# Tables for engines and urgencies in an attention and mixture-of-experts kernel

## The chip, the cores and the metric

The kernel runs on one core of one Trainium2 chip. The time is device microseconds of one execution of the whole program, median of several runs; smaller is better. The core has five engines with a queue each, worked off in order: TensorE (PE, matmul; its weight loads are shown as PEld), VectorE (DVE), ScalarE (ACT), GpSimd (POOL) and SyncE (SP, which here only issues DMAs). POOL issues DMAs too, here those that add into their destination. The profile is taken by the hardware profiler in one execution.

## The reference

Attention with 2 batches, 8 heads, 768 positions and 64 columns per head, local windows plus block summaries, then two mixture-of-experts layers. Cut to what matters:

```python
def _attn_ref(q, k, v):                    # each (2, 8, 768, 64)
    block, window = (32, 16)
    k_sum = k.reshape(B, H, nb, block, D).max(axis=3)
    v_sum = v.reshape(B, H, nb, block, D).mean(axis=3)
    scores_l = scale * np.matmul(q, k.transpose(0, 1, 3, 2))     # kept where |i - j| < window
    scores_s = scale * np.einsum('bhsd,bhnd->bhsn', q, k_sum) + np.log(block)
    a = softmax over [scores_l masked, scores_s]
    return np.matmul(a, np.concatenate([v, v_sum], axis=2))

def _moe_ref(x, domain_probs, w1, w2):     # x (1536, 512), 4 experts, 1024 hidden columns
    p = domain_probs / (domain_probs.sum(-1, keepdims=True) + 1e-09)
    for e in range(E):
        out += p[:, e:e + 1] * (np.maximum(x @ w1[e], 0.0) @ w2[e])

def _moe2_ref(x, w_gate, w1, w2):          # the same with 8 experts
    logits = x @ w_gate
    P = np.exp(logits - logits.max())      # then 8 rounds of row and column normalisation
    ...                                    # out += P[:, e:e + 1] * (relu(x @ w1[e]) @ w2[e])
```

Everything is computed in float32 precision: each operand of a large matmul is split into a high part, rounded for the matmul, and a low part, the difference, and three products are added.

## The kernel before, in words

**Stages.** The attention works on 8 pairs of heads, each in 3 groups of 4 windows. Per pair: load keys, queries, values and value windows (`add_loads`, SP's queue), transpose keys and queries on TensorE, copy the key windows out of PSUM, take the block maxima and spread them beside the windows (line 1139, `add_keys`), scale the queries (line 1166, `add_queries`), add up the values of a block (`add_values`). Per group (`add_group`): scores on TensorE (lines 1228 and 1234), row maxima (line 1250) and sums on DVE, exponentials on ACT (line 1256), the product with the reciprocal of the sums on POOL (line 1271), transposes (1280), a copy (1286), the product with the values (1295), a copy (1306). `add_x` turns the attention's result into seven operand combinations of Strassen's scheme with high and low parts (`hi_op`, line 468, on ACT; `lo_op`, lines 458 and 463, on DVE or POOL).

Then 96 steps follow, one for each of 48 quarters of experts (16 in the first layer, 32 in the second) and each half of the rows. A step has seven products of the first matrix (line 306, six matmuls of 384 columns each) and twice seven of the second (line 629, three matmuls each), 84 matmuls in all. Between them `add_hop` makes seven operands with high and low parts, and ACT and DVE empty the PSUM banks and add into accumulators (line 646 and the helpers in lines 241 to 247, which record the lines of `vsub`, `vadd` and `vmul`). Weights are loaded by SP; their combinations are made by casts on ACT (lines 486 and 499), subtractions on DVE and adding DMAs from POOL's queue (lines 502 and 515). At the border between the layers `add_turn` turns accumulators into the second layer's operands, `add_gate` and `add_sinkhorn` compute the gates and `add_scale` applies them, some steps later. At the end `add_out` combines the accumulators, transposes the result on TensorE (line 947), copies it from PSUM to stage buffers (DVE line 955 for odd tiles, ACT line 959 for even ones) and stores it.

**The order.** No instruction is issued where it is written. Each `op` call records an operation with its engine, a duration name, what it reads and writes, and a due time in steps; its number is its place in that order of calls (0 to 8223). At the end `run_work` plans them all: from the operations whose inputs are there in its plan it always takes the one that can start first, and among those that can start at the same time the one with the smallest due time, and issues it. So the order of every engine's queue is fixed when the program is built. The plan's durations are in the table `SPAN` (how long the engine is taken, and when the result is there), `HOP_WAIT` is added where a result goes to another engine, and operations marked as shared (`w[5]`) wait for each other, whether on DVE or on POOL:

```python
                    t = max(f, at[i], port) if w[5] else max(f, at[i])
                    ...
                    key = (t, w[3], i)        # w[3] is the due time
```

The engine of an operation is written out where it is made (`vop` for DVE, `aop` for ACT), with a few lists that move some to POOL: `XPOOL` for low parts in `add_x`, `VPOOL` and `KSPOOL` for pair 7.

Of the kernel before, what the change touches and what calls it, by code (L numbers as in the profile page):

```python
# [12 lines left out]
ALU = mybir.AluOpType  # L13
# [5 lines left out]
def local_global_attention_moe_moe(  # L19
# [299 lines left out]
    def relu(S, out, src, th, neg=False):  # L319
# [35 lines left out]
    HOP_WAIT = 0.12  # L355
# [26 lines left out]
    def run_work():  # L382
# [7 lines left out]
        free, avail, dma = {}, {}, 0.0  # L390
# [9 lines left out]
        for _ in range(n):  # L400
# [47 lines left out]
    def vop(fn, reads, writes, due, span="v", two=True, use=None):  # L448
        op("DVE", span, reads, writes, due, fn, two, use=use)

    def aop(fn, reads, writes, due, span="a", use=None):
        op("ACT", span, reads, writes, due, fn, use=use)

    def lo_op(eng, to, src, reads, writes, due, neg=False):
        def fn(e=nc.gpsimd if eng == "POOL" else nc.vector):
# [9 lines left out]
        op(eng, "p384" if eng == "POOL" else "v", reads, writes, due, fn, True)  # L465

    def hi_op(to, src, reads, writes, due, neg=False):
        aop(lambda: nc.scalar.mul(to(0), src, -1.0 if neg else 1.0), reads, writes, due, "ah")  # L468
# [58 lines left out]
    def add_first(n):  # L527
# [11 lines left out]
        def fork(out, src, kin, kout, due, by=1.0):  # L539
            aop(lambda: nc.scalar.mul(out, src, by), [kin], [kout], due)  # L540

        def gate(name, src, th, reads, due, two, neg=False):
            if plain(S):
                aop(lambda: relu(S, q[name], src, th, neg), reads, [name], due)
# [36 lines left out]
    def add_hop(n):  # L581
# [12 lines left out]
        def two(f, o, x, y, due):  # L594
            vop(lambda: f(q[o], q[x], q[y]), [x, y], [o], due)
# [24 lines left out]
    def add_second(n):  # L620
# [18 lines left out]
        def copy(out, kout, src, kin, due):  # L639
            aop(lambda: nc.scalar.copy(out=out, in_=src), [kin], [kout], due)  # L640
# [79 lines left out]
    def add_x(b, c, due):  # L720
# [7 lines left out]
        def two(f, out, x, y, reads, writes, d):  # L728
            vop(lambda: f(out, x, y), reads, writes, d)
# [23 lines left out]
    def add_turn(b, due):  # L753
        for c in range(KH):
# [13 lines left out]
            def two(f, out, x, y, kx, ky, ko, d):  # L768
                vop(lambda: f(out, x, y), [kx, ky], [ko], d)
# [18 lines left out]
    def add_scale(b, row, due):  # L788
        p0, p1_ = row[:, 0:HB], row[:, HB:BLK]
        for c in range(KH):  # L790
# [4 lines left out]
            def two(f, out, x, y, reads, ko):  # L795
                vop(lambda: f(out, x, y), reads, [ko], due)
# [756 lines left out]
```

## Time and profile before

| | |
|---|---|
| time, median of 3 runs | 1538.95 us (1538.51 to 1541.38) |
| span of the profiled execution | 1537.7 us, 26631 instructions |
| TensorE busy | 1508.6 us, 98% |
| DVE busy | 1376.9 us, 90% |
| ACT busy | 1131.5 us, 74% |
| POOL busy | 480.8 us, 31% |
| granted TensorE clock, mean | 0.997 |

For the profiled execution the page gives the span, from its first instruction to its last; its time outside of the span is not listed. A window row gives, for one stretch, the busy time of each engine with the number of its instructions, the granted clock of TensorE as a share of full speed, the mean busy share of the 16 DMA engines and their GB/s. Matmuls are pipelined, so that a busy TensorE need not be at its peak. In a timeline row the start is in microseconds from the start of the span; the second number is the duration, and behind it stand engine, line, operation, output and input, with the idle time ahead of it and what ended that in brackets. Successive operations of one engine overlap: the next one starts before the shown end of the one before.

### The profile page before, as it was taken

The numbers are of one execution on the slowest core, as the hardware profiler recorded it, in microseconds if no ns is written. First come the engines' busy times: TensorE is split into PE (matmuls) and PEld (weight loads), VectorE is DVE, ScalarE is ACT, GpSimd is POOL, SyncE is SP. The second block draws the span as 40 slices with busy tenths as digits, with TensorE's granted clock in tenths as the row PEclk, the third lists the DMA queues.
The fourth block names the chain that finished last, engine by engine and source line by source line (L and its number), as shares of the span: only waits on it lengthen the run. The fifth ranks groups of instructions, "written<-read, shape, count | busy, mean of one in ns | idle before, by whom it ended". The sixth has DMA issues, their size and how long they took to land.

```text
span 1537.7 us, 26631 instructions
## 1 busy us (share of the span) xinstructions
PE 1508.6 (98%) x9048; PEld 1483.7 (96%) x9048; DVE 1376.9 (90%) x2846; ACT 1131.5 (74%) x2455; POOL 480.8 (31%) x508
## 2 busy tenths in 40 slices
PE   7989999999999999999999999999999999999997
PEld 6779999999999988999999999999999999999997
DVE  7877989899989998999899899899989989989988
ACT  5888777777777788777677777777777767767765
POOL 3443323323322242343332332323323332332220
PEclk9999999999999999999999999999999999999999
DMA  9967667666666684687666666666666667667642
GB/s 222 218 123 136 120 128 133 125 129 119 125 133 121 123 148 80 113 174 144 119 121 136 121 117 131 127 121 126 129 116 132 126 114 138 122 110 140 122 68 90
DMA packets 199865, 197.56 MB, mean 128 GB/s; under 512 B 46496, under 2 KB 158000, under 8 KB 199728
## 3 DMA queue, kind: packets, MB, share of 16 engines
q0 software_dynamic: 83776, 117.47, 48.3%
q1 hardware_dynamic: 115952, 78.39, 18.0%
q8 instruction: 71, 1.16, 0.3%
q14 instruction: 66, 0.54, 0.1%
HBM read 73.97 MB, written 3.22 MB: 50 GB/s over the span
## 4 chain that ended last, share of the span: by engine, by line
PE 90%; DVE 6%; ACT 2%; issue 1%; DMA 0%; POOL 0%; SPq 0%; DVEq 0%; ACTq 0%
PE bank L306 44%; PE bank L629 43%; PE bank L1234 1%; DVE acc L241 1%; DVE hoph L463 1%; DVE acc L1125 0%; DVE acc L244 0%; PE bank L1295 0%; DVE sm L1262 0%; DVE quads L244 0%; DVE xlo L463 0%; DVE quads L323 0%; ACT s L1256 0%; PE bank L1198 0%; DVE xlo L458 0%
## 5 line engine op out<-in xcount | busy, mean ns | idle before, releaser
L629 PE MATMUL bank<-hoph,w2hi 128*128 128x384 f32 x2688 | 686.7, 336 | 5.0 <-ACT bank L640 2.2
L629 PEld LDWEIGHTS bank<-hoph,w2hi 128*128 128x128 f32 x2688 | 483.5, 188 | 10.9 <-ACT bank L640 5.2
L629 PE MATMUL bank<-hoph,w2lo 128*128 128x384 f32 x1344 | 449.3, 334 | 0.4 <-DVE w2lo L244 0.4
L468 ACT ACTIVATE hoph<-quads 128x384 fp32r<-128x384 f32 x672 | 336.9, 520 | 109.1 <-PE bank L629 65.9
L241 DVE TENSOR_TENSOR acc<-bank,acc 128x384 f32<-128x384 f32 x726 | 378.7, 550 | 29.8 <-PE bank L629 29.1
L306 PE MATMUL bank<-xhi,w1hi 128*128 128x384 f32 x1008 | 339.1, 336 | 2.3 <-ACT w1hi L486 1.8
L306 PE MATMUL bank<-xlo,w1hi 128*128 128x384 f32 x1008 | 338.1, 335 | 0.8 <-DVE xlo L463 0.6
L306 PE MATMUL bank<-xhi,w1lo 128*128 128x384 f32 x1008 | 337.6, 335 | 0.4 <-DVE w1lo L244 0.4
L515 POOL DMA_DIRECT2D raw<-raw x195 | 201.0, 1041 | 405.1 <-DMA raw<-raw 181.2
L463 DVE TENSOR_TENSOR hoph<-quads,hoph 128x384 fp32r<-128x384 f32 x582 | 311.5, 550 | 9.2 <-ACT hoph L468 4.5
L629 PEld LDWEIGHTS bank<-hoph,w2lo 128*128 128x128 f32 x1344 | 252.3, 188 | 0.7 <-DVE w2lo L244 0.7
L640 ACT COPY bank<-bank 128x384 f32<-128x384 f32 x384 | 181.4, 472 | 92.6 <-PE bank L629 88.0
L306 PEld LDWEIGHTS bank<-xhi,w1hi 128*128 128x128 f32 x1008 | 189.5, 188 | 4.9 <-ACT w1hi L486 2.1
L306 PEld LDWEIGHTS bank<-xlo,w1hi 128*128 128x128 f32 x1008 | 189.5, 188 | 1.5 <-DVE xlo L463 1.4
L306 PEld LDWEIGHTS bank<-xhi,w1lo 128*128 128x128 f32 x1008 | 189.6, 188 | 0.8 <-DVE w1lo L244 0.7
L640 ACT COPY acc<-bank 128x384 f32<-128x384 f32 x222 | 104.8, 476 | 106.7 <-PE bank L629 104.9
L515 POOL DMA_DIRECT2D xf<-xf x93 | 97.8, 1052 | 187.3 <-DMA xf<-xf 91.9
L502 POOL DMA_DIRECT2D w2lo<-raw x67 | 71.0, 1059 | 153.2 <-ACT w2lo L499 142.3
L599 DVE SCALAR_TENSOR_TENSOR quads<-quads 128x384 f32<-128x384 f32 x192 | 105.7, 551 | 1.6
L323 DVE SCALAR_TENSOR_TENSOR quads<-bank,pb 128x384 f32<-128x384 f32 x180 | 99.5, 553 | 6.2
L244 DVE TENSOR_TENSOR quads<-quads,bank 128x384 f32<-128x384 f32 x96 | 53.1, 553 | 57.4 <-PE bank L306 57.2
L244 DVE TENSOR_TENSOR quads<-quads 128x384 f32<-128x384 f32 x186 | 102.4, 551 | 1.8
(193 smaller groups left out, 1920.7 us busy)
## 6 DMA issues: line engine op xcount, KB each, us to landing
raw<-raw POOLq DMA_DIRECT2D x130, 256.0 KB, 3.8
raw<-in_moe_w_dram SPq DMA_DIRECT2D x66, 256.0 KB, 2.9
raw<-in_moe_w_dram SPq DMA_DIRECT2D x128, 128.0 KB, 2.9
xf<-xf POOLq DMA_DIRECT2D x62, 256.0 KB, 3.8
w2lo<-raw POOLq DMA_DIRECT2D x33, 384.0 KB, 4.9
w1lo<-raw POOLq DMA_DIRECT2D x32, 384.0 KB, 4.0
pb<-prow SPq DMA_DIRECT2D x24, 384.0 KB, 4.0
w2lo<-raw POOLq DMA_DIRECT2D x34, 256.0 KB, 3.8
```

What stands on the lines that cost most here:

```text
L241: (eng or nc.vector).tensor_tensor(out=out, in0=x, in1=y, op=ALU.add)
L244: (eng or nc.vector).tensor_tensor(out=out, in0=x, in1=y, op=ALU.subtract)
L306: nc.tensor.matmul(pm, l[:, s, cs_], x_of(b, c, r, x), start=first and i == 0, stop=i == n - 1, skip_group_check=True,)
L323: nc.vector.scalar_tensor_tensor(out=out, in0=src, scalar=0.0, in1=PB[S[1]][:, th * HB:(th + 1) * HB], op0=ALU.min if neg else ALU.max, op ...
L463: e.tensor_tensor(out=out, in0=src, in1=hi.bitcast(F32), op=ALU.subtract)
L468: aop(lambda: nc.scalar.mul(to(0), src, -1.0 if neg else 1.0), reads, writes, due, "ah")
L502: lambda: nc.gpsimd.dma_start(out=l, in_=src, accum_op=ALU.add),
L515: lambda o=o, x=x: nc.gpsimd.dma_start(out=o, in_=x, accum_op=ALU.add),
L599: nc.vector.scalar_tensor_tensor(out=q[o], in0=q[x], scalar=-1.0, in1=q[y], op0=ALU.mult, op1=ALU.subtract)
L629: nc.tensor.matmul(cut[bank], l[:, s, cols], hop_of(t, r), start=start and i == 0, stop=i == 2, skip_group_check=True,)
L640: aop(lambda: nc.scalar.copy(out=out, in_=src), [kin], [kout], due)
L1234: nc.tensor.matmul(pw[:, tt * KX:(tt + 1) * KX], bd[p][:, g * GT + tt].rearrange("x j q -> x (j q)"), kw[p][(g * GT + tt) // KT][:, (g * G ...
```

## The change

A table `MOVED` gives operations by number a new engine, and a table `SHIFT` adds to the due time of 286 operations (from -80.5 to +84.1 steps). For this `op` takes a list of alternatives (`others`), each with engine, duration name and function, and the helpers that make operations hand one over: a high part or a copy out of PSUM on DVE instead of ACT, a low part or an addition on POOL instead of DVE or the other way, scaled queries and key copies on ACT instead of DVE or the other way, the share product on DVE. The lists `VPOOL` and `KSPOOL` go, and in `add_out` all stage copies are on ACT unless the table names them. With the entries that name the engine an operation has anyway left out, and 4 stage copies added that change for that reason, 180 operations change their engine:

| numbers | where | ACT to DVE | DVE to POOL | DVE to ACT | POOL to DVE |
|---|---|---|---|---|---|
| 0 to 522 | attention | 24 | 17 | 13 | 11 |
| 523 to 755 | steps 0 to 3 | 15 | 4 | | |
| 2869 to 3169 | steps 30 to 33 | 3 | 8 | | |
| 3170 to 3579 | steps 33 to 37 | 17 | 17 | | |
| 3580 to 3921 | steps 38 to 41 | 13 | 20 | | |
| 8043 to 8216 | last steps and end | 6 | 8 | 4 | |

The 24 of the attention are 9 copies of transposed shares, 9 copies of the attention's result, 3 high parts, 2 key copies and one scaling; the 17 are 14 additions and low parts and 3 spreads; the 13 are 6 scalings, 5 key copies and 2 small copies; the 11 are 8 share products and 3 low parts. At the border the 33 from ACT are 18 high parts and 15 copies or gates out of PSUM, the 45 to POOL are low parts, additions and gate products.

Of the 286 new due times 84 belong to the attention (17 of them on SP's queue), 28 to steps 0 to 3, 149 to the border and 25 to the end. Besides, the plan takes TensorE as half as fast in the first 8.3 us of its work (`COLD`), `HOP_WAIT` is halved, and some durations are changed. What an operation computes stays as it is, and none is added or left out.

```diff
-        "vks": (0.6, 0.69), "vksw": (0.600001, 0.69), "vks2": (0.35, 0.42), "vkw": (0.7, 0.81), "vq": (1.0, 1.1),
+        "vks": (0.6, 0.69), "vksw": (0.35, 0.42), "vks2": (0.35, 0.42), "vq": (1.0, 1.1),
...
-        "a": (0.41, 0.48), "ah": (0.42, 0.52), "a512": (0.53, 0.63), "a768": (0.74, 0.84),
-        "as": (0.2, 0.26), "awg": (1.4, 1.46), "akw": (0.8, 0.91), "aq": (0.95, 1.04), "aexp": (1.05, 1.12),
+        "a": (0.38, 0.48), "ah": (0.42, 0.52), "a512": (0.53, 0.63), "a768": (0.74, 0.84),
+        "as": (0.2, 0.26), "awg": (1.4, 1.46), "aq": (0.95, 1.04), "aexp": (1.05, 1.12), "akw": (0.68, 0.8), "vhi": (0.28, 0.37), "vax": (0.36, 0.42), "vf": (0.45, 0.55), "v480": (0.57, 0.66), "vkw": (0.68, 0.77), "vmul": (0.36, 0.45),
...
-    HOP_WAIT = 0.12
+    HOP_WAIT = 0.06
+    COLD = 8.3
+    MOVED = {
+        "ACT": (
+            75, 79, 132, 136, 140, 271, 275, 327, 393, 397, 445, 449, 453,
+        ),
+        "DVE": (
+            39, 53, 61, 72, 92, 151, 171, 180, 189, 199, 201, 223, 225, 229, 240, 246, 258, 287,
...
+        "POOL": (
+            25, 30, 185, 190, 226, 230, 233, 236, 250, 251, 254, 256, 373, 378, 379, 381, 395, 447,
...
+    MOVED = {i: eng for eng, ids in MOVED.items() for i in ids}
+    SHIFT = {
+        19: 4.94, 43: 19.67, 48: 26.76, 65: 17.82, 67: 20.37, 68: 21.85, 69: 29.51, 70: 25.6,
...
+        484: 1.86, 489: 13.95, 496: -10.56, 497: -30.88, 499: -8.25, 500: 11.53, 501: 33.12,
...
-    def op(eng, span, reads, writes, due, fn, shared=False, take=None, use=None):
+    def op(eng, span, reads, writes, due, fn, shared=False, take=None, use=None, others=()):
         i = len(work)
+        due += SHIFT.get(i, 0.0)
+        for other in others:
+            if other[0] == MOVED.get(i):
+                eng, span, fn, shared = other
...
+            if eng == "PE":
+                cold = cold or t + COLD
+                extra = min(busy, max(cold - t, 0.0) / 2)
+                busy, late = busy + extra, late + extra
...
+    def by_vector(span, fn, shared=False):
+        return (("DVE", span, fn, shared),)
+
+    def by_scalar(span, fn):
+        return (("ACT", span, fn, False),)
+
+    def by_pool(span, fn):
+        return (("POOL", span, fn, True),)
...
-        op(eng, "p384" if eng == "POOL" else "v", reads, writes, due, fn, True)
+        if eng == "POOL":
+            op("POOL", "p384", reads, writes, due, lambda: fn(nc.gpsimd), True,
+               others=by_vector("v", fn, True))
+        else:
+            op("DVE", "v", reads, writes, due, fn, True,
+               others=() if neg else by_pool("p384", lambda: fn(nc.gpsimd)))
...
+        by = -1.0 if neg else 1.0
+        aop(
+            lambda: nc.scalar.mul(to(0), src, by), reads, writes, due, "ah",
+            others=by_vector("vhi", lambda: nc.vector.tensor_scalar_mul(to(0), src, by), True),
+        )
...
-            if t % 2:
-                vop(
-                    lambda i=i, o=o: nc.vector.tensor_copy(out=o, in_=full[i]),
-                    [bank], [ko], due, "v512", False,
-                )
-            else:
-                aop(lambda i=i, o=o: nc.scalar.copy(out=o, in_=full[i]), [bank], [ko], due, "a512")
+            aop(
+                lambda i=i, o=o: nc.scalar.copy(out=o, in_=full[i]), [bank], [ko], due, "a512",
+                others=by_vector("v512", lambda i=i, o=o: nc.vector.tensor_copy(out=o, in_=full[i])),
+            )
...
+            by_act = lambda c=scaled: c(nc.scalar.mul)
+            by_dve = lambda c=scaled: c(nc.vector.tensor_scalar_mul)
             if j:
-                aop(scaled, [("ptq", i, j)], [("bd", p, j)], d + 0.01, "aq", use=tk)
+                aop(by_act, [("ptq", i, j)], [("bd", p, j)], d + 0.01, "aq", use=tk, others=by_vector("vq", by_dve))
             else:
-                vop(scaled, [("ptq", i, j)], [("bd", p, j)], d, "vq", False, use=tk)
+                vop(by_dve, [("ptq", i, j)], [("bd", p, j)], d, "vq", False, use=tk, others=by_scalar("aq", by_act))
...
+            others=by_vector("v480", lambda: shares(nc.vector), True),
```

The other helpers (`fork`, `gate`, `two`, `copy`, the key copies, the spread, the small copies) get their alternatives in the same way.

## Rows read from the trace of the kernel before

**Rows 1.** Windows of the whole span; columns as in the section above.
```profile
0.00:60.00 60.00, 49.79 (x485) 43.19 (x485) 48.02 (x114) 41.26 (x114) 23.68 (x41) 1.00 1.06 218
60.00:80.00 20.00, 18.29 (x169) 16.03 (x170) 17.40 (x42) 16.43 (x47) 7.70 (x8) 0.91 1.00 206
80.00:100.00 20.00, 15.76 (x183) 13.45 (x182) 16.69 (x37) 16.68 (x52) 12.36 (x15) 0.98 0.60 115
100.00:120.00 20.00, 19.84 (x144) 18.35 (x143) 13.93 (x32) 17.01 (x41) 6.23 (x7) 0.93 0.56 122
120.00:560.00 440.00, 440.00 (x2531) 438.85 (x2530) 394.10 (x790) 328.84 (x692) 139.80 (x143) 1.00 0.67 127
560.00:600.00 40.00, 37.48 (x199) 31.82 (x199) 39.87 (x86) 35.91 (x83) 15.37 (x16) 1.00 0.73 126
600.00:660.00 60.00, 60.00 (x349) 58.13 (x348) 51.89 (x150) 48.70 (x105) 16.88 (x17) 1.00 0.55 104
660.00:700.00 40.00, 37.83 (x213) 36.52 (x213) 40.00 (x86) 27.72 (x59) 17.11 (x18) 1.00 0.89 171
700.00:1500.00 800.00, 800.00 (x4610) 800.00 (x4609) 723.93 (x1454) 580.19 (x1233) 240.43 (x245) 1.00 0.64 123
1500.00:1538.00 38.00, 29.62 (x179) 27.36 (x177) 31.10 (x63) 18.75 (x40) 1.19 (x1) 0.98 0.27 91
```

**Rows 2.** TensorE's waits, 0 to 104 us: total, times, longest (us).
```profile
PE bank L1096 <- DMA quads<-in_k_dram: 4.9, 1, 4.9
PE bank L1234 <- DVE kwb L1139: 2.4, 2, 1.9
PE bank L1280 <- POOL s L1271: 2.1, 3, 1.1
PE bank L1234 <- DVE kw L1139: 1.8, 2, 1.5
PE bank L306 <- ACT w1hi L486: 1.8, 1, 1.8
```

**Rows 3.** Windows of single microseconds: TensorE busy, granted clock, DMA share, GB/s.
```profile
62.00:63.00 1.00, 1.00 (x6) 0.50 1.11 233
...
100.00:101.00 1.00, 1.00 (x5) 0.50 0.85 249
```

**Rows 4.** Timeline of DVE ahead of the spread at 61.03 us.
```profile
57.00 1.11 DVE L1166 TENSOR_SCALAR acc<-bank 64x384 f32<-64x384 f32 x2
58.04 0.54 DVE L241 TENSOR_TENSOR acc<-acc 128x384 f32<-128x384 f32 x1
```

**Rows 5.** Groups by line, 0 to 104 us: busy us and mean ns.
```profile
L463 POOL TENSOR_TENSOR xlo<-acc,xhi 128x384 fp32r<-128x384 f32 x5 | 5.8, 1153 | 0.0
...
L1035 DVE CAST maskr<-acc 65x720 fp32r<-65x720 f32 x1 | 0.6, 597 | 0.3 <-POOL acc L998 0.3
```

**Rows 6.** Timeline of DVE and of POOL around 94 us.
```profile
93.86 1.82 DVE L244 TENSOR_TENSOR acc<-acc 128x384 f32<-128x384 f32 x2
...
94.09 1.17 POOL L1271 TENSOR_TENSOR s<-s,sm 128x480 f32<-128x480 f32 x1 [0.29 <-DVE sm L1266]
```

**Rows 7.** Timeline of DVE and TensorE near the end.
```profile
1528.00 0.69 DVE L955 COPY xf<-bank 128x512 f32<-128x512 f32 x1 [0.66 <-DMA out_dram<-xf]
1528.61 0.55 DVE L646 SCALAR_TENSOR_TENSOR acc<-bank,acc 128x384 f32<-128x384 f32 x1
1529.07 0.55 DVE L241 TENSOR_TENSOR acc<-bank,acc 128x384 f32<-128x384 f32 x1
...
1529.67 2.73 PE L947 MATMUL bank<-ident,acc 128*128 128x128 f32 x23 [0.99 <-DVE acc L241]
```

**Rows 8.** Values of the last pair: DMA issue to landing (us), issue, first reader.
```profile
vn<-in_v_dram SPq DMA_DIRECT2D x4, 384.0 KB, 5.9
...
69.14 2.27 SPq L1064 DMA_DIRECT2D vn<-in_v_dram  x1
...
84.78 1.49 PE L1198 MATMUL bank<-vn,sel 128*24 128x128 f32 x12
```

More of the change, by code (lines that the diff above doesn't have):

```diff
@@ L389, in run_work @@
         at = [0.0] * n
-        free, avail, dma = {}, {}, 0.0
+        free, avail, dma, cold = {}, {}, 0.0, 0.0
         port = 0.0
@@ L446, in run_work, with vop, aop, fn @@
         work.clear()
[L448 to L452, printed above, removed]
+    def vop(fn, reads, writes, due, span="v", two=True, use=None, others=()):
+        op("DVE", span, reads, writes, due, fn, two, use=use, others=others)
+    def aop(fn, reads, writes, due, span="a", use=None, others=()):
+        op("ACT", span, reads, writes, due, fn, use=use, others=others)
+    def by_vector(span, fn, shared=False):
[4 more added lines that the diff above has]
+        return (("POOL", span, fn, True),)
     def lo_op(eng, to, src, reads, writes, due, neg=False):
-        def fn(e=nc.gpsimd if eng == "POOL" else nc.vector):
+        def fn(e=nc.vector):
             out, hi = to(1), to(0)
@@ L639, in copy @@
         def copy(out, kout, src, kin, due):
-            aop(lambda: nc.scalar.copy(out=out, in_=src), [kin], [kout], due)
+            aop(
+                lambda: nc.scalar.copy(out=out, in_=src), [kin], [kout], due,
+                others=by_vector("vf", lambda: nc.vector.tensor_copy(out=out, in_=src)),
+            )
         def evac(k, bank, due):
@@ L728, in two @@
         def two(f, out, x, y, reads, writes, d):
-            vop(lambda: f(out, x, y), reads, writes, d)
+            vop(
+                lambda: f(out, x, y), reads, writes, d,
+                others=by_pool("p384", lambda: f(out, x, y, nc.gpsimd)),
+            )
         def one(i, src, key, d, neg=False):
@@ L795, in two @@
             def two(f, out, x, y, reads, ko):
-                vop(lambda: f(out, x, y), reads, [ko], due)
+                vop(
+                    lambda: f(out, x, y), reads, [ko], due,
+                    others=by_pool("p384", lambda: f(out, x, y, nc.gpsimd)),
+                )
             add_in(m2, m1, k2, k1, due - 0.5)
@@ L1106, in add_keys, with copies @@
             )
-            def copies(half=half, c0=c0, nh=nh, tk=tk):
+            def copies(copy, half=half, c0=c0, nh=nh, tk=tk):
                 pt = full[tk["bank"]]
@@ L1114, in copies @@
                 )
-                copy = nc.scalar.copy if half == 0 else nc.vector.tensor_copy
                 copy(out=t[half][:, t0:t0 + nw, 0:KW], in_=mid)
@@ L1142, in spread @@
                 )
-        op(
-            *(("POOL", "pks") if i in KSPOOL else ("DVE", "vksw")),
-            [("ks", p, 0), ("ks", p, 1)], [("kw", p, 2)], d + 0.03, spread,
+        vop(
+            spread, [("ks", p, 0), ("ks", p, 1)], [("kw", p, 2)], d + 0.03, "vksw", True,
+            others=(("POOL", "pks", lambda: spread(nc.gpsimd), False),),
         )
@@ L1181, in add_values, with rows @@
         tk = take_of(i)
-        def rows():
-            e = nc.gpsimd if i in VPOOL else nc.vector
+        def rows(e=nc.vector):
             vn = vns[p]
@@ L1189, in add_values @@
         if by == 2:
-            op(
-                *(("POOL", "p384") if i in VPOOL else ("DVE", "v")),
-                [("vn", p)], [("vn", p)], d - 0.01, rows, True,
+            vop(
+                rows, [("vn", p)], [("vn", p)], d - 0.01, "v", True,
+                others=by_pool("p384", lambda: rows(nc.gpsimd)),
             )
@@ L1206, in add_values @@
             [("pv", i)], [("vb", p)], d, "vvb", False, use=tk,
+            others=by_scalar("as", lambda: nc.scalar.copy(out=vbs[p][KW:KX], in_=full[tk["bank"]][KW:KX, 0:P])),
         )
@@ L1289, in add_group @@
             [("pa", w)], [("aT", w % 2)], d + 0.05, "a512", use=tks[1],
+            others=by_vector(
+                "v512",
+                lambda: nc.vector.tensor_copy(
+                    out=aT.rearrange("x t j q -> x (t j q)"), in_=bank[1]()[0:KX, :]
+                ),
+            ),
         )
@@ L1310, in add_group @@
             use=tks[2],
+            others=by_vector(
+                "vax",
+                lambda: nc.vector.tensor_copy(
+                    out=xfs[c][:, a, g * GW:(g + 1) * GW], in_=bank[2]()[:, 0:GW]
+                ),
+            ),
         )
@@ L1415, in local_global_attention_moe_moe @@
     LOPOOL = ()
-    VPOOL = (7,)
     VROWS = (1, 2, 7)
@@ L1422, in local_global_attention_moe_moe @@
     WAIT0 = 1
-    KSPOOL = (7,)
     XTOP = -4.2
```

66 lines of the change are left out of this document (47 added, 19 removed), and 49 rows, old and new, of tables (MOVED, SHIFT).

## The prediction

> **What bounds the kernel now.** I read the table of windows first [rows 1]: the reader should subtract TensorE's busy time from each stretch's length and look at which engine is full where it falls short. From 120 to 560 us and from 700 to 1500 us TensorE is busy for 440.00 of 440 and 800.00 of 800 us, at full granted clock. The kernel can gain nothing there except by fewer matmuls, and the change removes none. TensorE is idle in three places only. The attention (0 to 120 us): 10.2 + 1.7 + 4.2 + 0.2 = 16.3 us, of which 4.9 are the wait for the first keys [rows 2], so 11.4 can be attacked. The border (560 to 700 us): 2.5 + 2.2 = 4.7 us. The end: 8.4 us, of which 5.3 lie behind the last transposes (1529.67 + 2.73 = 1532.4 [rows 7], span end 1537.7), so 3.1.
>
> The clock adds to this: the mean granted clock is 0.91 in 60 to 80, 0.98 in 80 to 100 and 0.93 in 100 to 120 us [rows 1]. In the single microseconds [rows 3] it stands at 0.50, the 1.2 GHz level, with TensorE fully busy. The two spells follow the two longest idle stretches of TensorE (before 61.4 and before 98.8 us). In full-speed time they lose 0.09 x 20 = 1.8 us and 0.02 x 20 + 0.07 x 20 = 1.8 us. So the most that can be had is 11.4 + 3.6 + 4.7 + 3.1 = 22.8 us, 1.5% of the time.
>
> Then I read TensorE's waits [rows 2] and the order of the Vector engine ahead of the worst of them [rows 4].
>
> **The change, part by part.** An operation's number is its place in the order in which the program makes them; counts are from the tables and that order.
>
> Attention, numbers below 523. 13 operations go from DVE to ACT, 17 from DVE to POOL, 24 from ACT to DVE, 11 from POOL to DVE. So 30 leave DVE and 35 come, of similar lengths: DVE's 82 us in the first 100 [rows 1] stay about 82. This is no relief; only the order can gain. Two stalls can be followed.
> (a) At 61.4 us TensorE waits 1.9 us for the spread of the block maxima (line 1139) [rows 2]. Ahead of it on DVE stand the scaled queries of pair 5 (57.00, two instructions, 58.04 - 57.00 = 1.0 us to the next) and two additions of the x preparation (the first at 58.04; DVE starts the next such operation 0.46 us later [rows 4, 7]). The tables move the queries to ACT (number 327) and both additions to POOL (233, 236): 1.0 + 2 x 0.46 = 1.9 us leave the queue ahead of the spread, just the wait. With the idle time I count the clock spell behind it: 1.9 + 1.8 = 3.7 us. Late next is ACT, which now scales both halves of the queries; it is busy for 41.3 of the first 60 us [rows 1], so I let this hide.
> (b) Before 98.8 us TensorE waits 1.8 us for the cast of the first weights (line 486) and up to 1.1 for a share product on POOL (line 1271) [rows 2]. The cast of one slot and both its low parts get more urgent (496, 497, 499); the product goes to DVE (470), where 480 columns should take 0.46 x 480 / 384 = 0.6 us against 1.17 on POOL [rows 6], an estimate from those two rows. 1.8 + 0.5 = 2.3, with the second spell 4.1 us.
> The other 11.4 - 1.9 - 2.3 = 7.2 us of idle time are many short waits; I take no net change, bounds 3 us either way. Planning TensorE as cold touches the first 8.3 us of its work; the longest wait there is 1.5 us [rows 2], so it is worth 0 to 1.5; I take 0. Later loads are among the moved urgencies (17 on SP's queue); what they could cost is a rival below. Attention: 7.8 us.
>
> Steps 0 to 3 (523 to 755): 15 operations ACT to DVE, 4 DVE to POOL. DVE has 6 us free in 100 to 120 [rows 1] and the 15 cost it at most 15 x 0.46 = 6.9 less 1.8: nothing.
>
> Border, 2869 to 3921 (steps 30 to 41). 45 operations go from DVE to POOL, 33 from ACT to DVE (18 high parts, 15 copies out of PSUM). DVE loses 45 x 0.46 = 20.7 us. A high part read from SBUF has no row on DVE; bounds are 0.3 (a cast of 720 columns took 0.597 [rows 5], so 384 about 0.32) and 0.46. I take 0.32, the nearer form: 18 x 0.32 + 15 x 0.46 = 12.7. Net -8.0 of DVE's 131.8 us in 140. In the last stretch, where DVE is busy 40.00 of 40, 20 leave and 13 come (7 high parts, 6 copies): -9.2 + 5.0 = -4.2 us against 2.2 of idle TensorE. In 560 to 600, 8 leave and 3 come: -3.7 + 1.1 = -2.6 against 2.5, but ACT is at 35.9 of 40 there, so I count half. 2.2 + 1.2 = 3.4. What comes to POOL has no row in the border, where POOL only issues DMAs now; 384 columns took it 1.15 us in the attention [rows 5]. 45 x 1.15 = 52 us come to its 49 in 140 us: they fit, but each stands in order behind DMA issues that wait for an earlier transfer or a cast, and TensorE reads many of them. I take 0.4 off: 3.0 us, bounds 0 and 4.7.
>
> End, from 8043. 8 operations DVE to POOL, 5 high parts and a stage copy ACT to DVE, 4 stage copies DVE to ACT. At 1528.00 a stage copy on DVE starts after 0.66 us of waiting for a store to free its buffer, and the last evacuations stand behind it (1528.61, 1529.07), then the last transposes (1529.67) [rows 7]. Without the copy the evacuations start about 0.6 earlier. DVE's net is -8 x 0.46 - 4 x 0.61 + 5 x 0.32 + 0.61 = -3.9 us. I take 1.0 of the 3.1 us, bounds 0 and 3.1.
>
> The hop of 0.06 in the plan and the shorter ACT copy reorder all steps, also the 1240 full microseconds (85 steps of 84 matmuls, each 800 / 4610 = 0.174 us [rows 1]). Measured, one hop is 1529.67 - (1529.07 + 0.55) = 0.05 us [rows 7], so the new value is the truer. Cost 0 to 2.5 us (one product of each step late by 0.03); I take 0, since TensorE shows no idle time there to grow from.
>
> Sum: 7.8 + 3.0 + 1.0 = 11.8 us off. The page gives the span of the profiled execution, 1537.7; the median of the runs is 1.3 above. I keep that difference: 1538.95 - 11.8 = 1527.
>
> **The port that DVE and POOL share.** At 93.86 two subtractions on DVE took 1.82 us while POOL multiplied from 94.09 for 1.17 [rows 6]; undisturbed, two take 0.46 + 0.55 = 1.0. So a collision costs DVE 0.8 us, more than the 0.46 that a moved operation saves it. The Trainium skill (SBUF — State Buffer, section "SBUF: two separate sides") calls the shared port pair an exclusive lock, held for the whole instruction, and its page Perfetto Trace Analysis ("Optimizing Scalar/DVE Operations") warns that moving work between these two engines might not help. By that rule the moves to POOL in the border would be worth nothing or less; the collision at 93.86 agrees with the lock. It is the rival on the slow side.
>
> **Rivals.**
> 1. The loads bind the attention. For: the DMA share is 1.00 or more up to 80 us [rows 1]. Against: it is 0.60 after that, and the last pair's values, issued at 69.14 and landing some 5.9 us later, are read at 84.78 [rows 8], some 9 us of room, more than the 7.8. If the later loads use it up, attention gives 1 to 3 us and the total about 1534 (3 + 1 + 1 off).
> 2. Slower: the port. In border and end 53 operations go to POOL. If all collide, DVE pays 53 x 0.8 = 42 against 24 saved, with 15 for what comes from ACT: +33 us, of which its free time in 560 to 700 (140 - 131.8 = 8.2) takes 8. The border and end then grow by up to 25 us, less 7.8 in the attention: about 1556 at worst. It decides at the share of collisions where 42 x share = 24 - 15 + 8 = 17: 40%. At 70% the growth is 12, and the time about 1543. Against: the planner lets no such pair overlap in its plan, and DVE has evacuations out of PSUM to do meanwhile.
> 3. The hop: if TensorE waited 0.15 us in each of the 85 full steps, 12.8 us would eat the gain: 1540. Against: DVE is busy 90% there and TensorE never waits.
> 4. The tables do not do what they say: the waits only change places, since an engine's order is fixed and the chip's times differ from the plan's by more than the waits are long. Then 1538 or 1539.
>
> **How the numbers follow.** 0.2% is 3.1 us, about what a measurement of this kernel tells from no change. Forecast 0.64 (1521 to 1533). Loads 0.16, of which 0.13 faster and 0.03 the same. Port 0.09: 0.06 slower, 0.03 the same. Hop 0.04: half each. No effect 0.07: the same. Faster 0.64 + 0.13 = 0.77; same 0.15; slower 0.08. The range takes the bounds of the unknown terms downwards (3 + 1.5 + 1.7 + 2.1 = 8.3, hardly all at once: 1520) and the loads' rival upwards: 1520 to 1537. Some 0.15 lie above it and 0.04 below.
>
> **What would show it.** Right: in the after profile TensorE's idle time in the attention falls from 11.4 to about 7, the clock spells near 62 and 100 us are gone, the border shows under 2 us idle with POOL busy some 50 us longer, and the last transposes start near 1518. Wrong: DVE pairs of 1.8 us beside POOL operations in the border, TensorE waiting for low parts made on POOL, new idle time between 120 and 560, or loads landing just before their readers.

## The result and the profile after

The changed kernel takes 1556.07 us (1553.68 to 1557.56, four runs) against 1538.87 us of the kernel before beside it: a ratio of 1.0105, interval 1.0091 to 1.0120. It is slower by 17 us where 12 us less were forecast. Ratios here and below are worked out from the single undisturbed runs, so that they can lie up to 0.1% off the quotient of the medians; one of e2's five runs took 5275.72 us and is left out. The span of the profiled execution is 1553.1 us (before 1537.7).

To find the place, take from both traces the start of every matmul of the experts' products (lines 306 and 629, 84 per step) and subtract the start of the product of the same number. These differences are of one execution each:

| | after minus before, us |
|---|---|
| step 3.5 | -2.3 |
| step 30 | -1.9 |
| step 36 | +2.1 |
| step 38 | +8.2 |
| step 39.5 | +12.4 |
| step 42 | +16.3 |
| step 94 | +17.4 |
| last of them | +16.1 |

So the attention gave back 2.3 us, the border (steps 30 to 42) took 18.2, the full steps ahead of it 0.4 and those behind it 1.1, and the end returned 1.3 (2.0 by the end of the span). The windows of the changed kernel, to be laid beside [rows 1] (columns as there), say the same:

```profile
0.00:60.00 60.00, 50.02 (x490) 43.62 (x490) 49.09 (x110) 43.61 (x121) 25.63 (x46) 1.00 1.06 223
60.00:80.00 20.00, 16.88 (x157) 14.73 (x158) 15.73 (x35) 13.93 (x38) 10.84 (x12) 0.91 0.97 196
80.00:100.00 20.00, 17.08 (x194) 14.72 (x193) 17.96 (x39) 15.54 (x52) 12.15 (x13) 1.00 0.53 103
100.00:120.00 20.00, 19.75 (x152) 18.81 (x151) 18.55 (x43) 16.89 (x36) 10.02 (x10) 1.00 0.67 144
120.00:560.00 440.00, 439.53 (x2526) 437.97 (x2525) 393.58 (x797) 324.16 (x680) 146.44 (x148) 1.00 0.67 127
560.00:600.00 40.00, 36.12 (x196) 32.48 (x195) 37.39 (x76) 34.53 (x80) 19.53 (x20) 0.96 0.67 117
600.00:660.00 60.00, 58.21 (x335) 55.84 (x334) 55.66 (x147) 39.50 (x84) 33.37 (x33) 1.00 0.52 99
660.00:700.00 40.00, 32.91 (x170) 30.09 (x168) 38.44 (x59) 20.85 (x43) 25.24 (x27) 0.95 0.78 149
```

TensorE's idle time before 120 us is 9.98 + 3.12 + 2.92 + 0.25 = 16.3 us, what it was. In 660 to 700 us it is idle for 7.1 us instead of 2.2. DVE there is nearly as busy as before (38.4 of 40 us, before 40.0) but with 59 instructions for 86: it does less and takes almost as long. POOL is busy for 25 us where it was for 17.

Waiting is not all of it. From step 30 to step 42 (first the kernel before, then the changed one) TensorE is idle for 14.8 us instead of 4.7, and for as many products it is busy for 7.9 us longer, at a granted clock of 0.96 instead of 1.00. So of the 18 us some 10 are idle time and some 8 a slower TensorE:

```profile
540.00:735.00 195.00, 190.30 (x1074) 181.09 (x1073) 180.65 (x420) 154.06 (x332) 69.85 (x73) 1.00 0.72 134
```

```profile
538.00:751.00 213.00, 198.22 (x1072) 187.86 (x1072) 197.80 (x406) 140.07 (x298) 116.42 (x117) 0.96 0.64 120
```

What a busy DVE does in that stretch is seen in its timeline with POOL's, ACT's and TensorE's (start, duration, engine, line; line 546 is [rows 5]'s 463, line 247 the gates' product):

```profile
674.93 4.96 DVE L546 TENSOR_TENSOR hoph<-quads,hoph 128x384 fp32r<-128x384 f32 x2 [0.75 <-ACT hoph L558]
...
675.33 2.26 POOL L247 TENSOR_TENSOR acc<-acc,pb 128x384 f32<-128x384 f32 x2
...
677.85 1.61 POOL L244 TENSOR_TENSOR acc<-acc 128x384 f32<-128x384 f32 x1
678.08 0.44 PE L739 MATMUL bank<-hoph,w2hi 128*128 128x384 f32 x1 [2.04 <-DVE hoph L546]
...
679.92 0.49 ACT L633 ACTIVATE quads<-bank 128x384 f32<-128x384 f32 x1 [3.50 <-DVE hoph L546]
```

Two low parts took DVE 4.96 us; two take 1.0 alone. Meanwhile POOL ran three operations that the change gave it. TensorE waited 2.0 us for one of the low parts, ACT 3.5. It looks like the collision of [rows 6], but the two low parts were held through three POOL instructions, not through one. Summing what each DVE operation takes above the median of its own form in the same execution (counted from 0.06 us on) gives 25.9 us from 540 to 760 us in 25 places, and none in the kernel before.

### The profile page after: what moved, and what is told of

Its sections match the earlier page's. It is cut to its first block, busy times and chain, and to the rows that moved or that the text cites. A ratio compares the mean times of both kernels' runs of the same rounds, so it can differ in the third digit from the quotient of the medians.

```text
span 1553.1 us, 26618 instructions
## 1 busy us (share of the span) xinstructions
PE 1515.7 (98%) x9048; PEld 1488.4 (96%) x9048; DVE 1384.8 (89%) x2833; ACT 1114.5 (72%) x2402; POOL 547.6 (35%) x574
## 4 chain that ended last, share of the span: by engine, by line
PE 86%; DVE 7%; ACT 3%; issue 1%; DMA 1%; POOL 1%; DVEq 0%; SPq 0%; POOLq 0%; ACTq 0%
PE bank L306 42%; PE bank L739 42%; DVE acc L241 1%; ACT s L1381 1%; DVE hoph L546 1%; DVE quads L709 0%; DVE sm L1387 0%; PE bank L1359 0%; DVE quads L244 0%; DMA w2lo<-xf 0%; DVE quads L323 0%; DVE acc L1247 0%; DMA out_dram<-xf 0%; DVE nm L1375 0%; PE bank L938 0%
## 5 line engine op out<-in xcount | busy, mean ns | idle before, releaser
L558 ACT ACTIVATE hoph<-quads 128x384 fp32r<-128x384 f32 x643 | 319.3, 520 | 132.6 <-PE bank L739 76.8
L607 POOL DMA_DIRECT2D raw<-raw x195 | 206.5, 1074 | 353.0 <-DMA raw<-raw 141.2
L546 DVE TENSOR_TENSOR hoph<-quads,hoph 128x384 fp32r<-128x384 f32 x546 | 302.5, 567 | 3.1 <-ACT hoph L558 2.6
L751 ACT COPY bank<-bank 128x384 f32<-128x384 f32 x373 | 175.5, 471 | 123.5 <-PE bank L739 110.4
L607 POOL DMA_DIRECT2D xf<-xf x93 | 101.1, 1087 | 165.9 <-DMA xf<-xf 62.0
L633 ACT ACTIVATE quads<-bank 128x384 f32<-128x384 f32 x189 | 91.9, 487 | 38.9 <-PE bank L306 27.7
L709 DVE SCALAR_TENSOR_TENSOR quads<-quads 128x384 f32<-128x384 f32 x192 | 109.8, 572 | 1.2
```

The source lines that it names most:

```text
L546: e.tensor_tensor(out=out, in0=src, in1=hi.bitcast(F32), op=ALU.subtract)
L558: lambda: nc.scalar.mul(to(0), src, by), reads, writes, due, "ah",
L607: lambda o=o, x=x: nc.gpsimd.dma_start(out=o, in_=x, accum_op=ALU.add),
L633: lambda: nc.scalar.mul(out, src, by), [kin], [kout], due,
L709: nc.vector.scalar_tensor_tensor(out=q[o], in0=q[x], scalar=-1.0, in1=q[y], op0=ALU.mult, op1=ALU.subtract)
```

## The experiments

Three explanations stood at the start: P, the port that DVE and POOL share; Q, POOL's queue, where moved operations stand in order with the adding DMAs; S, the shifted urgencies. For every run the table gives the ratio of its time to that of before beside it, the growth of the border (matmul starts at step 30 and step 42, each minus before's) and the sum by which DVE operations are lengthened in 540 to 760 us. Four runs whose border is planned exactly as before give +0.0 to +0.4 us; finer differences of the border are nothing. Border and lengthening are of the one profiled execution, the ratio of all runs; where they differ, the ratio counts. In e12 above all the profiled execution was the slowest of four (1554.24 us, median 1551.32).

| run | ratio, interval | border, us | DVE lengthened, us |
|---|---|---|---|
| the change | 1.0105 (1.0091 to 1.0120) | +18.2 | 25.9 |
| e1, without the 45 border moves to POOL | 1.0045 (1.0029 to 1.0060) | +7.6 | 0.4 |
| e2, border without tables | 1.0039 (1.0025 to 1.0053) | +6.6 | 0 |
| e3, the 45 moves and the constants alone | 1.0145 (1.0131 to 1.0159) | +17.5 | 22.3 |
| e5, constants alone | 1.0077 (1.0065 to 1.0090) | +6.5 | 0.1 |
| e7, hop 0.06 alone | 1.0056 (1.0043 to 1.0070) | +4.3 | 0 |
| e8, constants, hop 0.12 | 1.0052 (1.0038 to 1.0066) | +1.3 | 0 |
| e9, hop 0.18 alone | 1.0046 (1.0031 to 1.0062) | +6.0 | 0.3 |
| e10, tables of attention and end, old constants between | 0.9985 (0.9977 to 0.9994) | +0.2 | 0 |
| e22, the same again | 0.9981 (0.9973 to 0.9990) | 0.0 | 0 |
| e13, tables of the attention alone | 1.0005 (0.9997 to 1.0014) | +0.1 | 0 |
| e20, tables of the end alone | 0.9999 (0.9990 to 1.0007) | +0.4 | 0 |
| e16, e10 with the 45 moves | 1.0084 (1.0067 to 1.0101) | +12.2 | 17.7 |
| e17, idle memsets on POOL | 1.0028 (1.0016 to 1.0040) | +2.8 | 0.1 |
| e18, a waiting copy on POOL | 1.0035 (1.0023 to 1.0047) | +5.1 | 0 |
| e12, both | 1.0065 (1.0050 to 1.0081) | +13.5 | 0 |
| e21, idle additions on POOL | 1.0105 (1.0091 to 1.0119) | +17.2 | 19.1 |
| e11, additions and the waiting copy | 1.0099 (1.0085 to 1.0113) | +16.8 | 10.5 |

### Taking the change apart

e1 leaves the 45 numbers out of the table for POOL, e2 all table entries from 2869 to 3921:

```diff
-            542, 566, 647, 698, 2884, 2886, 2982, 2987, 3006, ..., 3857, 3860, 3866, 8058, ...
+            542, 566, 647, 698, 8058, ...
```

> The changed kernel without the 45 moves from DVE to POOL at the border (steps 30 to 41); all other moves, urgencies and plan constants stay. Theories: P, the port: the 45 operations block DVE (lengthened DVE operations sum to 24 us in 600 to 760 us of the changed kernel, none there before). Q, POOL's queue: the 45 stand in order with the DMA issues, and both come late for TensorE. S, the shifted urgencies and the reordering reorder the border badly, whatever engine the 45 are on. P and Q: the 18 us that the border grew by fall to at most 4 (DVE takes back 20.7 us and keeps the 12.7 from ACT, 144.5 in 140 us): 1538 to 1542. S: still above 1550.

> The changed kernel without any move or urgency between numbers 2869 and 3921; attention, steps 0 to 3, end and plan constants as in the change. By the landmarks of the changed kernel (attention -2.3, steady steps +1 to +1.5, end -1.3) all theories of the border expect 1536 to 1538. If the border loses time even so (by the halved hop or by what came earlier), it comes out above 1541.

e3 keeps those 45 moves as the only entries that change an engine, e5 empties both tables in the same sense (seven entries stay that give operations the engine they have in the kernel before), so that only the constants of the plan differ from before:

> No move and no urgency except the 45 moves from DVE to POOL at the border; plan constants as in the change. P and Q: the border loses most of the 18 us by these alone: 1550 to 1558; somewhat less under P if DVE's relief (20.7 us, and nothing from ACT) pays for part of the collisions: 1545. S: about 1539.

> No move and no urgency at all; only the plan constants of the change (hop 0.06 for 0.12, TensorE cold for the first 8.3 us, the shorter ACT copy and the other changed durations). P, Q and S have no effect here: 1538 to 1540 if the hop costs nothing in the full steps; the hop's rival wants up to 1551 (0.15 us in 85 steps).

The 45 moves cost the border 18.2 - 7.6 = 10.6 us by e1 and 17.5 - 6.5 = 11.0 by e3: S falls for them, P or Q holds. The other border entries (33 operations from ACT to DVE, 149 urgencies) are worth e1 minus e2, +1.0 us. But the times missed what was expected: e1 lies between the forecasts of P and Q and that of S, e3 lies above its range, and e2 and e5 were to lose nothing in the border: without any border table the border still loses 6.5 us, and the constants alone make the kernel 0.77% slower. Of the 12.3 us by which the span of e5's profiled execution is longer, 6.5 lie in the border, 1.4 in the full steps behind it, 2.1 ahead of step 30 and 2.3 from step 94 on. The windows of e5 and, below it, of a kernel with before's plan in the border (e10) show that TensorE works 131.9 of 140 us instead of 135.0, and loses another 1.05 us in the full steps:

```profile
560.00:700.00 140.00, 131.88 (x733) 122.03 (x732) 127.36 (x309) 108.27 (x237) 49.89 (x52) 1.00 0.66 124
700.00:1500.00 800.00, 798.95 (x4593) 796.49 (x4592) 713.10 (x1456) 586.45 (x1234) 242.19 (x246) 1.00 0.65 123
```

```profile
560.00:700.00 140.00, 134.97 (x756) 125.92 (x754) 131.73 (x321) 111.95 (x244) 49.23 (x52) 1.00 0.70 130
700.00:1500.00 800.00, 800.00 (x4610) 800.00 (x4610) 724.21 (x1454) 580.72 (x1234) 241.63 (x246) 1.00 0.65 123
```

### Is the new hop wrong, or is any new plan worse?

e7 and e9 change one number of the kernel before, `HOP_WAIT`, from 0.12 to 0.06 and to 0.18. e8 takes every constant of the change but the hop.

> The kernel before with one number changed, the plan's hop 0.06 for 0.12. V: the halved hop makes the plan too tight, and that costs the 12 us of the constants: about 1550. A: the shorter ACT copy does it: about 1540 here. R: any new plan loses the good order of the border, whatever the number: somewhere from 1540 to 1552.

> The kernel before with the hop 0.18, as far above 0.12 as the change went below. V: no loss, 1537 to 1541. R: a loss as at 0.06, 1542 to 1552.

> All plan constants of the change except the hop, which stays 0.12; no move, no urgency. V: about 1540. A: about 1550. R: 1540 to 1552.

Smaller and larger hop lose alike, 4.3 and 6.0 us in the border. So a shorter hop isn't the point (V falls): a new value orders the border anew, and both new orders are worse than the one that before has. Two values don't show that every other order is worse. e8 loses only 1.3 us there; its 1.0052 lies mostly ahead of step 4, where its profiled execution was 7 us behind. e10 tests this from the other side: the change's tables and constants outside of 756 to 8042, before's constants inside.

```diff
-    HOP_WAIT = 0.06
+    OUTER = lambda i: i < 756 or i >= 8043
+    HOP_WAIT = lambda i: 0.06 if OUTER(i) else 0.12
...
+        if span == "a" and not OUTER(i):
+            span = "a_before"          # (0.41, 0.48)
```

> The change's tables for attention, steps 0 to 3 and end with its constants there; from number 756 to 8042 no move, no urgency, and the hop and the ACT copy of before. By landmarks the tables are worth 2.3 in the attention and 1.3 at the end. If the constants alone spoil the border (V or A): 1535 to 1537. If any change of the plan upstream spoils it (R): 1540 to 1548.

Its border is in before's order, operation for operation, and loses 0.2 us. So it isn't any change upstream that spoils the border, as R had it; the constants do it where they order the border itself. The kernel takes 1536.67 us, 0.15% less than before: faster than both. A second series gave 1536.66 us and 0.9981:

> The mixed kernel (tables for attention and end, the constants of before between) a second time, beside new runs of before. If its gain is real: 0.06 to 0.23% less again. If the attention's clock spells and the occasion made it: within 0.1% of before.

The same tables in two halves, e13 with the attention's alone, e20 with the end's alone:

> The tables for the attention and steps 0 to 3 alone (numbers below 756) with the change's constants there; from there on everything as before. By the prediction's term 7.8 us less; by the landmark of the changed kernel 2.3 less; by what the tables gain in the kernel's own plan (3.1 at step 6) 3 less. If the clock's spells decide, between 1 us more and 4 less.

> The kernel before with the change's tables and constants from number 8043 on alone; the order of all else as in before. By the mixed kernel (-3.6 to -0.9 us for attention and end together) and by the attention's tables alone (-0.5 to +2.2): 1.3 to 3 us less. If the gain was the attention's: within 1 us.

Neither half alone differs from before by more than its interval, and together they gain 0.15 to 0.19%. The ends of the halves' intervals (0.03% and 0.10% less) add up to 0.13%, which is inside the intervals of the whole (from 0.06% and 0.10% on) and short of its middle; where the 2.5 us of the whole come from stays open.

### The port or the queue

e16 puts the 45 moves on the good border of e10:

> The kernel with tables for attention and end and the constants of before between (1536.67 us in its runs) with the 45 border moves from DVE to POOL added. P: the moves cost what they cost in the changed kernel, 9 to 12 us, and replanning the border another 0 to 5: 1546 to 1554. If they cost only in a border that the constants had spoilt already: 1537 to 1541.

12.2 us against 0.2: the price of the moves hardly depends on the constants. It holds both the port and the queue, so the next kernels leave all operations of before where they were, in before's order, and give POOL only idle work beside each of the 45: e17 four memsets of 188 columns, e18 a copy of one column of the operation's result (so POOL waits for it), e12 both, e21 two additions of 188 columns, e11 additions and copy. The edit, with the four versions of `beside` in one and the shapes of the additions left out:

```diff
+    def beside(i):
+        out = made[i]                                    # what operation i writes
+        nc.gpsimd.tensor_copy(out=both[:, 0:1], in_=out[:, 0:1])      # e11, e12, e18
+        for _ in range(4):
+            nc.gpsimd.memset(both, 0.0)                               # e12, e17
+        for _ in range(2):
+            nc.gpsimd.tensor_tensor(out=both, in0=o2, in1=o2, op=ALU.add)    # e11, e21
...
             fn()
+            if i in BESIDE:
+                beside(i)
```

> The kernel before, every operation on its engine and in its place; beside each of the 45 border operations POOL gets three more instructions in its queue: a copy of one column of that operation's result (so that they start when it is done), and two additions of 188 columns whose result nobody reads. P, the port: DVE operations beside them are lengthened by 0.5 us and more, together by 12 to 25 us in 560 to 740 us, and the border, where DVE has some 8 us free, grows by 5 to 15: 1544 to 1554. Q, POOL's queue alone: DVE operations keep their length, the adding DMAs come late, and the time is as with the memsets of the next run.

> The same with four memsets of 188 columns in the place of the two additions: the same places in POOL's queue, but apart from the one column nothing is read from SBUF. P, if the lock is for reads: two-input DVE operations are not lengthened, and the time is within 3 us of before. P, if writes lock as well: as the additions. Q: as the additions, both 3 us or more above before.

> The four memsets beside each of the 45 operations without the copy that waits for the operation's result: POOL is taken as long, in the same places of its queue, but waits for nothing more. O, the time that POOL is taken: 1548 to 1553, as with the copy (1551.3). W, its waiting in order: within 4 us of before.

> The copy of one column alone, that waits for the operation's result, without memsets: POOL is hardly taken (45 x 0.3 us or less), but waits. W: 1546 to 1552. O: within 3 us of before. If both are needed, some 3 to 6 us in each of the two runs.

> The two additions of 188 columns without the copy. Against the memsets without the copy this is the port alone: DVE operations lengthened by about 10 us in 560 to 740 us as before (some 45 of them by 0.2), and 2 to 6 us more time than the memsets.

Groups by line, 560 to 755 us (busy us, mean ns): DVE's low parts in the kernel before, then DVE's low parts and POOL's idle work in e12 (memsets and copy), in e21 (additions), and the memsets of e17.

```profile
L463 DVE TENSOR_TENSOR hoph<-quads,hoph 128x384 fp32r<-128x384 f32 x79 | 41.9, 545 | 1.7 <-ACT hoph L468 1.6
```

```profile
L481 DVE TENSOR_TENSOR hoph<-quads,hoph 128x384 fp32r<-128x384 f32 x73 | 38.7, 546 | 3.4 <-ACT hoph L486 3.2
L368 POOL MEMSET both<- 128x188 f32 x170 | 43.4, 255 | 9.9
L366 POOL COPY both<-hoph 128x1 f32<-128x1 f32 x27 | 19.4, 718 | 14.4 <-DVE hoph L481 14.2
```

```profile
L482 DVE TENSOR_TENSOR hoph<-quads,hoph 128x384 fp32r<-128x384 f32 x73 | 43.2, 607 | 1.3 <-ACT hoph L487 1.2
L367 POOL TENSOR_TENSOR both<-ones 128x188 f32<-128x188 f32 x84 | 78.2, 930 | 4.4
```

```profile
L366 POOL MEMSET both<- 128x188 f32 x168 | 57.3, 341 | 8.0
```

e12's memsets leave DVE's mean at 546 ns (545 in the kernel before) and take 255 ns each; additions raise DVE's to 607 and are themselves stretched to a mean of 930 ns (shortest 494, longest 5925). Not all of that stretch is the port: 32 of e21's 90 additions begin while POOL still issues a DMA, as do 32 of e17's 180 memsets, and those 32 memsets take 736 ns on average, the other 148 only 256. The 58 additions that begin beside no such issue take 701 ns on average. The Trainium skill (SBUF — State Buffer, section "Who interferes with whom") has a DVE instruction with two SBUF inputs contend with a POOL instruction that reads SBUF and not with one that only writes it; the 256 and the 701 ns agree, and so does DVE's own length.

So P is shown: e21 has e17's places in POOL's queue and nothing to wait for, and costs 17.2 us in the border where e17 costs 2.8 (by the ratios of all runs 16 and 4 us). That was more than expected: 2 to 6 us above e17, with some 10 us of lengthening, for which 19.1 came.

Q is shown as a path, but not as a price that is free of the port. e17, which takes POOL's time without a wait, costs 2.8 us and lengthens DVE by 0.1. e12 lengthens no DVE operation either and costs 13.5 in the profiled execution, where at most 3 were expected if only reads lock. By the ratios it costs 10 us, and its halves e17 and e18 4.3 and 5.4, so that the two just add up. But the copy of e18 and e12 reads SBUF, and e18 shows what comes of it. All of its 5.1 us arise in one place. A copy on POOL takes 5.07 us beside a row of DVE operations (last section); the adding DMA behind it goes out at 689.60; TensorE needs what it adds and waits 3.3 us, and from 694 to 697 us its granted clock is 0.50, the 1.2 GHz level. POOL and TensorE, then one of those microseconds (columns as in [rows 3]):

```profile
684.59 5.07 POOL L366 COPY both<-hoph 128x1 f32<-128x1 f32 x1 [1.29 <-DVE hoph L479]
689.60 1.20 POOL L518 DMA_DIRECT2D w2lo<-raw  x1
...
693.51 0.44 PE L645 MATMUL bank<-hoph,w2lo 128*128 128x384 f32 x1 [3.28 <-DMA w2lo<-raw]
```

```profile
694.00:695.00 1.00, 1.00 (x5) 0.50 1.23 193
```

So an instruction that stands in POOL's queue does delay TensorE through the DMA behind it, and here it was the port that made it stand. For e12 the delay comes in several small pieces; from the waits of POOL, ACT and DVE, 560 to 755 us (total, times, longest):

```profile
POOL both L366 <- DVE hoph L481: 14.2, 9, 4.0
ACT w1hi L504 <- DMA raw<-in_moe_w_dram: 4.6, 2, 2.4
DVE acc L245 <- POOL both L366: 2.7, 1, 2.7
```

POOL stands waiting for low parts of DVE, and its copies, 0.18 us at the least, take 718 ns on average in this group (23 of all 45 begin while POOL issues a DMA, the others take 0.41 us on average: some of both). The DMAs that the kernel before issues at 577.7 to 592.6 us go out 8.5 to 10.6 us later, while TensorE is only about 2 us behind. ACT then waits for a load of raw weights with its cast (4.6 us; in the kernel before that wait doesn't appear in the border); that the load is late because the adding DMAs read its buffer late is argued from the order, not shown. A part is the test's own: DVE waits 2.7 us to overwrite what the copy still has to read, and TensorE loses some 3 us right behind it.

The additions alone (e21, 17.2) do what the whole change did, and the waiting copy with them (e11, 16.8, slightly above what was expected in time) adds nothing. In the changed kernel POOL waits for its low parts in the same way, over the same stretch:

```profile
POOL hoph L546 <- ACT hoph L558: 15.4, 9, 3.6
```

How the change's own 10.6 to 12 us divide between the port's direct price on DVE and the queue isn't settled: the two overlap, and the port also holds up POOL.

## Why the prediction was wrong, step by step

**The hop and the constants: the term that was left at 0.** I bounded them at 0 to 2.5 us, with the argument that TensorE has no idle time in the full steps to grow from. For the full steps that was right: e5 loses 1.4 us from step 42 to 94. The step that failed is that I costed the hop there alone. The constants order the border anew as well, and in the border TensorE has idle time to grow from (4.7 us, [rows 1]). Measured for all constants (e5): 6.5 us there, 11.9 on the whole kernel; for the hop alone (e7) 4.3 and 8.6. That 0.06 is nearer to the measured 0.05 us of one hop [rows 7] was no reason for a gain: 0.18 costs nearly as much (e9: 6.0 in the border, 7.1 on the whole). Rival 3 priced the hop at 1540 but put it in the wrong place, the 85 full steps.

**The border's moves: -3.0 forecast, +10.6 to +12 measured.** Two steps failed. First, "they fit, but each stands in order" with 0.4 us taken off: the queue was treated as a question of room (52 us into POOL's free time). Room alone is cheap: e17's memsets take 57.3 us of it and cost 2.8. But one instruction that stands 5 us in that queue costs 5.1 (e18). Second, the argument against the port, that the planner lets no such pair overlap: it holds in the plan only, and on the chip 25 DVE places were lengthened by 25.9 us. The relief of DVE, -8.0 us by the sum, is less than a third of that lengthening. Besides, the border's sum has no term for the clock, which the attention's has: 8 of the border's 18 us are TensorE at a lower granted clock.

**Rival 2 named the right mechanism with too small a chance.** It had 0.8 us for a collision and 42 us if all collide; measured are 1.0 us and 25.9, some 62% of that. Its rule, lengthening less what is saved and what is free, gives 25.9 - 17 = 9 us of growth for the change. That this is near the 10.6 is luck: for e3, where nothing comes from ACT, the same rule gives 22.3 - 20.7 - 8.2, less than nothing, and the moves cost 11.0. The sum over the border doesn't decide; where TensorE waits for the lengthened operation does, as for the low part at 678.08. That its worst case, 1556, is the measured time is chance: it is made of other terms, without the constants and with 7.8 us of gain ahead.

**Attention: -7.8 forecast.** The profiled execution shows -2.3, but one execution can't carry that. Seven profiled executions have before's order up to there (before itself, e11, e12, e17, e18, e20, e21) and reach step 3.5 at -2.9 to +1.6 us against before (mean +0.3); seven have the change's order (the change, e1, e2, e10, e13, e16, e22) and lie between -2.3 and +1.7 (mean -0.6). So the tables are worth about 0.9 us, less than the spread of one order. The granted clock is part of what spreads: with the change's order it is 0.91 in 60 to 80 us of the changed kernel, 0.95 in e2 and 0.83 in e13, with TensorE busy for 16.9, 17.7 and 16.6 us. The clock spells that I counted into two stalls (3.6 us) aren't tied to those stalls alone. As for stall (a): the waits for the spread (line 1263 now) fell from 2.4 + 1.8 us [rows 2] to 0.7 + 0.6, as worked out. But TensorE now waits in the same place for a share product (waits to 125 us, then DVE's timeline before it):

```profile
PE bank L1407 <- POOL s L1395: 3.7, 5, 2.0
PE bank L1407 <- DVE s L1395: 3.4, 2, 3.1
PE bank L1359 <- DVE kw L1263: 0.7, 1, 0.7
PE bank L1359 <- POOL kwa L1263: 0.6, 1, 0.6
```

```profile
59.21 0.53 DVE L244 TENSOR_TENSOR acc<-acc 128x384 f32<-128x384 f32 x1
59.70 0.56 DVE L541 SCALAR_TENSOR_TENSOR xlo<-acc,xhi 128x384 fp32r<-128x384 f32 x1
60.17 0.55 DVE L546 TENSOR_TENSOR xlo<-acc,xhi 128x384 fp32r<-128x384 f32 x1
60.64 0.35 DVE L559 TENSOR_SCALAR xhi<-acc 128x384 fp32r<-128x384 f32 x1
60.91 0.65 DVE L1387 TENSOR_REDUCE sm<-s 128x4 f32<-128x484 f32 x1
61.48 0.55 DVE L546 TENSOR_TENSOR xlo<-acc,xhi 128x384 fp32r<-128x384 f32 x1
61.94 0.65 DVE L1395 TENSOR_TENSOR s<-s,sm 128x480 f32<-128x480 f32 x1
```

The product, moved from POOL to DVE (number 307), stands there behind five operations of the x preparation, one of them a high part moved from ACT (the 0.35 us at 60.64). The step that failed is "late next is ACT": I looked for what is late next on the engine that took the queries and not on DVE itself, which got as many operations as it gave. Stall (b): the 1.8 us for the first weights' cast are gone, and one share product on POOL makes TensorE wait 2.0. Rival 4, that the waits only change places, is what came true here.

**End: -1.0 forecast, -1.3 measured** by the last products of the changed kernel, of e10, e20 and e22 alike (1.3 to 1.4). The time of e20, which has this part alone, shows no such gain (0.9999, 0.9990 to 1.0007), though its interval allows it. **Steps 0 to 3: 0 forecast**, and between the first and the fourth step nothing is lost (-2.1 and -2.3).

**What would show it** was mostly answered by the list under wrong: DVE pairs beside POOL operations (4.96 us instead of the 1.8 that I had named), idle time in 120 to 560 (0.5 us, small), low parts on POOL standing late. Behind its first wait (4.7 us, before 4.9) TensorE waits in the attention for a transfer for 0.2 us only (up to 125 us), so rival 1 didn't decide.

## What to carry over

Before moving work to POOL, look at what else stands in its queue: an instruction that stands there holds back every DMA behind it, and one that reads SBUF holds up DVE or is held up by it, so price both, with a wait and a port term, and don't ask only whether POOL has room. Where TensorE begins to wait, look at its granted clock behind the wait too: the change lost nearly as much by the clock as by the waits. A constant of a planner is an edit of every stage that it orders; cost it in the stage with the least slack, and keep the old value where the old order is good, as e10 does. Where an effect is no larger than the spread of the same order from execution to execution, only repeated timing decides, not one trace.

## What the runs showed of the hardware

The port that DVE and POOL share can hold off either side for several instructions of the other in a row. POOL's copy of one column takes 0.18 us at the least. In e18, POOL's copy at 684.59 (shown above) took 5.07 us. DVE's timeline beside it, from its second microsecond on:

```profile
685.79 1.01 DVE L248 TENSOR_TENSOR acc<-acc,pb 128x384 f32<-128x384 f32 x2
686.72 0.54 DVE L242 TENSOR_TENSOR acc<-acc 128x384 f32<-128x384 f32 x1
687.19 0.54 DVE L245 TENSOR_TENSOR acc<-acc 128x384 f32<-128x384 f32 x1
687.66 1.95 DVE L248 TENSOR_TENSOR acc<-acc,pb 128x384 f32<-128x384 f32 x4
689.54 0.55 DVE L242 TENSOR_TENSOR acc<-bank,acc 128x384 f32<-128x384 f32 x1
```

The copy ended at 689.66, when the row of DVE operations with two inputs from SBUF was over and one with an input from PSUM (`bank`) ran. Four more copies of e18 took over 1.5 us beside such a row (at 547.48, 574.69, 580.82 and 679.77 us), and each ended just behind the start of a DVE operation that reads `bank`. So an instruction of POOL beside such a row was starved, and its queue with it; with the parts changed, the two low parts at 674.93 above were held through three POOL operations. Neither was in my price of 0.8 us for a collision.
